# Two of seven inner tiles of the MLP by seven products ahead of the attention, and the output projection by seven products

## The chip, the cores and the metric

The kernel runs on one core of one Trainium2 chip. Its time is the device time of the core in microseconds (us); shorter is better. TensorE (PE) multiplies matrices into PSUM; VectorE (DVE), ScalarE (ACT) and GpSimd (POOL) work element by element; SyncE (SP) mostly issues DMAs, and so does ACT here for some stores. Each engine works through its own queue in order, and waits in it for what other engines or DMAs have to finish.

## The reference

One sequence of 2048 rows of width 1024, all in float32. The rows are normalized; attention with 32 heads of width 32 and an MLP with 3584 inner columns both start from the normalized rows, and the MLP's output gates the attention's.

```
xn = layernorm(x)
q, k, v = split(xn @ wqkv)                          # wqkv 1024 x 3072, 32 heads of 32
s = softmax(q k^T / sqrt(32)) v, heads joined, @ wo # wo 1024 x 1024
h = xn @ w1 + b1                                    # w1 1024 x 3584
g = silu((h * tanh(softplus(h))) @ w2)              # mish; w2 3584 x 1024
out = x + s * g
```

## The kernel before, in words

**Matmuls.** A float32 operand is split into a high part (a rounded copy, made by ACT, `copy`) and a low part (what is left, made by DVE or POOL, `low`). A product of two such operands is three matmuls: high by high, high by low, low by high (`THREE`). The unit of work is a matmul of 128 x 128 by 128 x 512 columns. The product of probabilities and v alone runs unsplit, four times slower for each pass, with four column groups at once.

**Stages.** (1) Rows are normalized and transposed, and v is made (`v_group`, L354); meanwhile POOL splits the first seven tiles of W1. (2) q and k (`product`, L798) are made by seven products in place of eight: the pair of a q and a k tile of 128 columns, times a pair of row chunks of 512, is taken as a 2 x 2 product of blocks in Winograd's form, with the inner dimension halved. Sums of weight blocks are made by POOL (`w_sum`, L554), split by ACT and DVE into pieces (`piece`), and sums of row blocks are prepared in stage 1. There are 16 jobs of seven products of twelve matmuls: eight column tiles for each of two pairs of row chunks. `q_load` brings a job's weights two jobs ahead; `SEQ` is the order of products; `out_` copies and splits a finished block and stores it to DRAM. After each product, `later.tick()` runs what was put off by some products. In the last five jobs the first head's scores (`s_mm`) run in between.

(3) The attention and the MLP run together, in an order that a planner works out on the host before the kernel is built (`Plan`). Five streams of PE work are given with a due time each (`key`): the scores s, by which a row's maximum is found (L920, DVE takes the maximum at L926); the transposed scores t (L1007), which ACT turns into exponentials p (L285); h (L1213), 24 matmuls for each of 28 inner tiles and 4 row chunks; y (L1303), the MLP's second product; and the output's first row chunk. The planner keeps a clock for every engine and takes on PE the operation that is ready and due first. Rings give the buffers: seven p tiles, one z, three `act`, five W2 halves (`w2`), two whole W1 tiles (`w1`). For each head, POOL adds up the p tiles into z (L1036), 15 additions; p times v runs on PE in three groups (`GROUPS`, L1054); then z's column sums (`zp`, L1080) and the division (`norm`), and the head's rows go to DRAM (`ot`, L1102). `mish` is five steps of ACT and seven of DVE for each h tile of 128 x 512, ending in a split `act`. W2 comes raw for the first row chunk, is split by ACT and POOL (L296) and stored for the other three; so are 21 tiles of W1. y is summed in `yacc` by DVE (L1325) and stored to `ys` at the end of each chunk (L1330).

(4) The output (L1402): 16 row tiles by two halves of columns, 24 matmuls each, 768 in all, followed by two DVE steps per block (L1495, L1496: times the gate, plus x). Its first eight blocks are the planner's fifth stream: their first half uses heads 0 to 15, stored long before, and their second half the rest. The gate is Silu of y, by ACT.

Of the kernel before, what the change touches and what calls it, by code (L numbers as in the profile page):

```python
# [18 lines left out]
P = 128  # L19
# [9 lines left out]
SLOW, UNTIL = 1.25, 700.0  # L29

W2_Q = 0
NS = H * NT
HK = KT // 2

# [6 lines left out]
PS, ACTS, W2S, Y0, Y1 = 7, 3, 5, 0.6, 0.17  # L41

AHEAD, BEHIND = 1.5, 1
# [4 lines left out]


# [3 lines left out]
LEAN = ("11875111088588544715468766661886741604280263056046486663654100588"  # L53
        "24308444562028442608686254255866647666488105044664767708017872000")
# [35 lines left out]
class Plan:  # L90
# [6 lines left out]
    SEM, SWITCH, LAND, RATE = 0.07, (0.25, 0.13), 2.0, 0.25e6  # L97
# [25 lines left out]
    def ready(self, op):  # L123
# [8 lines left out]
        for name in op.take:  # L132
            if not self.rings[name]:
                return None
            when = max(when, min(self.rings[name])[0] + self.SEM)
# [15 lines left out]
    def do(self, op, when):  # L151
# [8 lines left out]
        elif e == "SP":  # L160
            self.dma = max(self.dma, start) + op.bytes / self.RATE
            op.end = self.dma + self.LAND
        else:
            op.end = start + took
            took -= self.AHEAD[e]
# [65 lines left out]
def body(ctx: ExitStack, tc: tile.TileContext, x, wqkv, wo, w1, b1, w2, out):  # L231
# [17 lines left out]
    w1s = [dram.tile([P, 2, KT, P], F32R, name=f"w1s{i}") for i in range(FT)]  # L249
# [10 lines left out]
    nc.vector.memset(one, 1.0)  # L260
    zero = consts.tile([P, 1], F32, name="zero")
# [38 lines left out]
    def w1_tile(name):  # L300
        return w1p.tile([P, 2, KT, P], F32R, tag="w1", name=name, bufs=2)
# [132 lines left out]
    def split_w(w, raw, job=False):  # L434
        for half in range(2):
            r = slice(half * 4, half * 4 + 4)
            if job:
                nc.gpsimd.tensor_copy(w[:, 0, r], raw[:, r])
            else:
                copy(w[:, 0, r], raw[:, r])  # L440
            low(nc.gpsimd if job else nc.vector, w[:, 1, r], raw[:, r], w[:, 0, r])
# [4 lines left out]
    def w1_early():  # L446
# [3 lines left out]
        if f > 1:  # L450
            move(w1s[f - 2], early_w1.pop(f - 2)[1])
        if f < W1_V:
            raw = vp.tile([P, KT, P], F32, tag="x", name=f"w1e{f}", bufs=XB)
            nc.sync.dma_start(raw, w1[:, f * P:(f + 1) * P].rearrange("(k p) f -> p k f", p=P))
            early_w1[f] = [raw, None]
        if 0 < f <= W1_V:
            raw, _ = early_w1[f - 1]
            early_w1[f - 1][1] = w = w1_tile(f"w1p{f - 1}")
            split_w(w, raw, True)
# [75 lines left out]
    nc.sync.dma_start(bias1, b1.rearrange("(f p) -> p f", p=P))  # L535

    PAIRS = ((2, 3), (0, 1))
    A11, S2, A12, S3, S1, A22, S4 = range(7)
    NQ = 2 * KT
    raws, sums, pieces = {}, {}, {}  # L540

    def q_load(q, tiles, halves=range(2)):
        raws[q] = tiles
        for half in halves:
            col = half * D + q % KT * P
            nc.sync.dma_start(tiles[half], wqkv[:, col:col + P].rearrange("(k p) f -> p k f", p=P))
# [1014 lines left out]
```

## Time and profile before

| | before |
|---|---|
| median of 3 runs | 3362.83 us (3362.34 to 3363.39) |
| span of the profiled execution | 3358.0 us |
| PE busy | 3345.8 us |
| POOL busy | 2524.7 us |
| DVE busy | 2510.8 us |
| ACT busy | 2056.5 us |
| DMA, read and written in HBM | 352.55 and 144.97 MB |

The profiled execution's own time is known by its span, from the first to the last instruction; the runs' times are taken around the whole launch. In the profile, a group's row gives the line, the engine, the operation, the tile written and those read, how many there are, their busy time and the mean of one, and after the second bar the time in which the engine stood idle before them and what ended it. Matmuls overlap, so a mean of 391 ns says little; the step from one to the next says more. A row of the chain of work gives start, length and what ran. "DMA to landing" is from the issue to the data's arrival.

### The profile page before, as it was taken

What the parts mean: (1) busy time and instruction counts of PE and PEld (TensorE: products, weight loads), DVE (VectorE), ACT (ScalarE), POOL (GpSimd) and SP (SyncE); (2) the same over time, 40 slices, a digit from 0 to 9 for tenths busy, and PEclk for the clock granted to TensorE, in tenths of its full rate; (3) what the DMA queues carried; (4) which work ended last, traced back from release to release, by engine and by line L of the source; (5) the groups of instructions that cost most, each with busy time, mean ns of one, the idle gap of its engine ahead of it and who ended that gap; (6) DMA issues with size and microseconds to landing.
All of it is one profiled execution on the core that took longest, in us unless ns stands there. A gap on an engine that the chain in (4) does not pass through costs nothing.

```text
span 3358.0 us, 45795 instructions
## 1 busy us (share of the span) xinstructions
PE 3345.8 (100%) x16886; PEld 2458.4 (73%) x16886; DVE 2510.8 (75%) x3987; ACT 2056.5 (61%) x3313; POOL 2524.7 (75%) x750
## 2 busy tenths in 40 slices
PE   9999999999999999999999999999999999999999
PEld 7888887776777677776777677777677777767787
DVE  6665678877877778887888688888787888886542
ACT  5233436676766666666676666666667666667621
POOL 1323546999999887888888988888888898889800
PEclk9999999999999999999999999999999999999999
DMA  7865745454565643343335334333344433433482
GB/s 248 298 204 181 242 146 183 140 184 152 169 191 172 221 126 115 105 122 114 101 117 179 111 101 126 101 112 116 101 151 139 116 106 112 130 108 107 140 304 83
DMA packets 291460, 501.56 MB, mean 149 GB/s; under 512 B 88138, under 2 KB 151114, under 8 KB 269130
## 3 DMA queue, kind: packets, MB, share of 16 engines
q1 hardware_dynamic: 271524, 456.95, 43.8%
q10 hardware_dynamic: 19712, 41.69, 3.3%
q8 instruction: 133, 2.18, 0.3%
q14 instruction: 91, 0.75, 0.1%
HBM read 352.55 MB, written 144.97 MB: 148 GB/s over the span
## 4 chain that ended last, share of the span: by engine, by line
PE 96%; DMA 1%; DVE 1%; POOL 1%; issue 0%; ACT 0%; SPq 0%; ACTq 0%; POOLq 0%; DVEq 0%
PE y L1303 18%; PE h L1213 18%; PE t L1007 14%; PE s L920 13%; PE pv L1054 13%; PE op L1402 5%; PE v L354 5%; PE q_y L798 3%; PE q_z L798 2%; PE q_x L798 2%; PE zp L1080 1%; PE s L700 0%; POOL z L1036 0%; PE pt L423 0%; DMA w2r<-in_B_w_dram 0%
## 5 line engine op out<-in xcount | busy, mean ns | idle before, releaser
L1036 POOL TENSOR_TENSOR z<-z,p 128x2048 f32<-128x2048 f32 x448 | 2067.7, 4615 | 98.0 <-ACT p L285 72.9
L285 ACT ACTIVATE p<-t,zero 128x512 f32<-128x512 f32 x2048 | 1377.1, 690 | 560.1 <-PE t L1007 535.7
L926 DVE TENSOR_REDUCE mx<-s 128x1 f32<-128x512 f32 x1984 | 1322.3, 685 | 382.7 <-PE s L920 371.9
L1303 PE MATMUL y<-w,act 128*128 128x512 f32 x2688 | 920.3, 391 | 0.8 <-DVE yacc L1325 0.5
L1007 PE MATMUL t<-qstack,kstack 128*128 128x512 f32 x2048 | 799.1, 393 | 1.1 <-ACT p L285 0.7
L920 PE MATMUL s<-kstack,qstack 128*128 128x512 f32 x1984 | 772.6, 393 | 0.2 <-ACT p L285 0.2
L1213 PE MATMUL h<-xr,w 128*128 128x512 f32 x2016 | 697.7, 391 | 0.4 <-DMA xr<-xs 0.4
L1303 PEld LDWEIGHTS y<-w,act 128*128 128x128 f32 x2688 | 503.3, 188 | 114.3 <-issue 6.7
L1007 PEld LDWEIGHTS t<-qstack,kstack 128*128 128x128 f32 x2048 | 383.8, 188 | 114.8 <-issue 18.0
L1054 PE MATMUL pv<-p,v 128*32 128x512 f32 x4096 | 459.3, 594 | 0.0
L920 PEld LDWEIGHTS s<-kstack,qstack 128*128 128x128 f32 x1984 | 369.6, 188 | 118.5 <-issue 32.1
L1213 PEld LDWEIGHTS h<-xr,w 128*128 128x128 f32 x2016 | 378.3, 188 | 81.2 <-issue 3.4
L1325 DVE TENSOR_TENSOR yacc<-yacc,y 128x512 f32<-128x512 f32 x416 | 282.7, 680 | 82.6 <-PE y L1303 81.5
L1054 PEld LDWEIGHTS pv<-p,v 128*32 128x32 f32 x4096 | 123.3, 110 | 282.7 <-issue 281.1
L1036 POOL TENSOR_TENSOR z<-p,p 128x2048 f32<-128x2048 f32 x32 | 148.1, 4628 | 185.2 <-PE zp L1080 146.6
L1213 PE MATMUL h<-xc,w 128*128 128x512 f32 x672 | 231.3, 391 | 1.3 <-DMA w<-w1s 1.0
L354 PE MATMUL v<-vw,xc 128*128 128x512 f32 x768 | 179.7, 392 | 1.2 <-ACT xc L288 0.7
L354 PEld LDWEIGHTS v<-vw,xc 128*128 128x128 f32 x768 | 142.7, 188 | 32.0 <-ACT xc L288 1.4
L1213 PEld LDWEIGHTS h<-xc,w 128*128 128x128 f32 x672 | 125.9, 188 | 30.5 <-issue 2.5
L288 ACT ACTIVATE act<-h 128x512 fp32r<-128x512 f32 x112 | 66.6, 595 | 88.2 <-DVE h L1262 87.0
L798 PE MATMUL q_y<-xc,wq 128*128 128x512 f32 x480 | 115.3, 389 | 0.0
L798 PEld LDWEIGHTS q_y<-xc,wq 128*128 128x128 f32 x480 | 90.0, 188 | 18.8
(149 smaller groups left out, 2947.4 us busy)
## 6 DMA issues: line engine op xcount, KB each, us to landing
w<-w1s SPq DMA_DIRECT2D x91, 1024.0 KB, 5.4
w<-w2s SPq DMA_DIRECT2D x168, 512.0 KB, 4.0
w2s<-w SPq DMA_DIRECT2D x56, 512.0 KB, 4.0
qstack<-qs SPq DMA_DIRECT2D x96, 256.0 KB, 6.3
kstack<-ks SPq DMA_DIRECT2D x96, 256.0 KB, 5.8
w1s<-w SPq DMA_DIRECT2D x21, 1024.0 KB, 5.8
qs<-qst ACTq DMA_DIRECT2D x32, 512.0 KB, 4.1
ks<-qst ACTq DMA_DIRECT2D x32, 512.0 KB, 3.7
```

Of the source, the lines that this page charges most:

```text
L285: nc.scalar.activation(out_, in_, fn, bias=zero if bias is None else bias, scale=scale)
L354: nc.tensor.matmul(ps, xc[t // 4][k // HK][:, a, k % HK, (t % 4) * P:(t % 4 + 1) * P], vw[i, k // 2][:, b, k % 2], start=n == 0, stop=n == ...
L798: nc.tensor.matmul(ps, w[:, a, k], xx[:, b, k], start=m == 0 and i in (0, 1, 4), stop=m == 3 * HK - 1, skip_group_check=i not in (0, 1, 4))
L920: nc.tensor.matmul(sp_, qst[h % 3][:, qt * P:(qt + 1) * P], kst[h % 3][:, kc * 512:(kc + 1) * 512], start=True, stop=True)
L926: nc.vector.reduce_max(tiles["mx"][:, qt, kc:kc + 1], tiles[qt, kc], axis=AX.X)
L1007: nc.tensor.matmul(tp, kst[h % 3][:, kt * P:(kt + 1) * P], qst[h % 3][:, c * 512:(c + 1) * 512], start=True, stop=True)
L1036: nc.gpsimd.tensor_tensor(zs[h], pts[T - 1] if kt == 1 else zs[h], pts[T], ALU.add)
L1054: nc.tensor.matmul(pv[h][c * DH:(c + 1) * DH, :], vt[h][:, k, :], pts[T - kt + k][:, c * 512:(c + 1) * 512], start=k == 0, stop=k == NT - 1)
L1213: nc.tensor.matmul(t["h"], w1t[n][:, a, k], xts_[c][k // HK][:, b, k % HK], start=i == 0, stop=i == 3 * KT - 1)
L1303: nc.tensor.matmul(t["y"], acts[n][:, p, s * P:(s + 1) * P], w2t[m_][:, q], start=j == 0 and i == 0, stop=j == YB - 1 and i == 2)
L1325: nc.vector.tensor_tensor(ya, ya, t["y"], ALU.add)
L1402: nc.tensor.matmul(ps[t, dh], ohl[t // 4, k][:, a, s * P:(s + 1) * P], wt[k][:, b, r], start=k == 0 and i == 0, stop=k == KT - 1 and i == 2)
```

## The change

Three things, and what they carry along.

**Seven products for part of h.** Of 28 inner tiles, those with number 2 or 5 modulo 7 (`MADE`, eight) leave the attention. They are made in stage 2: two such tiles are the two column blocks of a job, in the place that a q and a k tile have, and eight jobs (four pairs by two pairs of chunks) stand between the two halves of the q/k jobs. Of each block, `out_` stores to DRAM (`hs`) the two things that mish needs, e = exp(min(h, 12)), as exp(12 - relu(12 - h)), and (e + 2) e h. In the attention such a tile is loaded (`h_load`, ring `hb`) and its mish starts from there, with four steps of ACT and four of DVE. The other tiles' mish takes the minimum on ACT (`a0`) in place of DVE (`d1`).

**W2 and the W1 buffers.** 38 of the 56 half-tiles of W2 are split in stage 2 (`ahead`, one each three or four products: load, copy by ACT, low by POOL, store). In the attention, the lows of the remaining W2 halves and W1 tiles move from POOL to DVE. The room of two whole W1 tiles becomes four quarters: in the attention two of them hold W1 in halves (`HALVES`), one holds `e`, one the loaded h. The ring of v shrinks from two to one, that of `act` grows to four.

**The output by seven products.** Eight jobs of 256 rows by 1024 columns, seven products of twelve matmuls each, after the attention. wo's block sums are made by POOL and split as the planner's fifth stream; the rows' sums by DVE and POOL. The planner's due times leave `END` = 30 us between the end of t and the end of all, `SLOW` is 1.0 in place of 1.25, and the string `LEAN`, which shifts the planner's choices in each 21 us, is another.

```diff
-SLOW, UNTIL = 1.25, 700.0
-W2_Q = 0
+SLOW, UNTIL = 1.0, 700.0
+NP = NT // 2
+MADE = [f for f in range(FT) if f % 7 in (2, 5)]
+KEPT = [f for f in range(FT) if f not in MADE]
-PS, ACTS, W2S, Y0, Y1 = 7, 3, 5, 0.6, 0.17
-AHEAD, BEHIND = 1.5, 1
+PS, ACTS, W2S, Y0, Y1 = 7, 4, 5, 0.6, 0.17
+AHEAD, BEHIND, END, H0 = 1.5, 1, 30.0, 1.0
+LOWS, W2_Q = "DVE", 38
...
-    def w1_tile(name):
-        return w1p.tile([P, 2, KT, P], F32R, tag="w1", name=name, bufs=2)
+    def quarter(i, name, shape=(P, 2, HK, P), dtype=F32R):
+        return w1p.tile(list(shape), dtype, tag=f"quarter{i}", name=name)
...
-    NQ = 2 * KT
+    NM = len(MADE) // 2
+    JOBS = [("q", t) for t in range(KT)] + [("h", g) for g in range(NM)] * 2 + [("q", t) for t in range(KT)]
+    NQ = len(JOBS)
+    TURN_Q, OFF = NQ // 2, NM
...
     def out_(q, half, chunk_, src):
+        kind, t = JOBS[q]
         st = sp.tile([P, 2, 512], F32R, tag="qst", name=f"qst{q}_{half}_{chunk_}", bufs=4)
+        if kind == "h":
+            f = MADE[2 * t + half]
+            dst = hs[f].rearrange("h p n -> p h n")[:, :, chunk_ * 512:(chunk_ + 1) * 512]
+            e, num = st[:, 0].bitcast(F32), st[:, 1].bitcast(F32)
+            def first():
+                act(num, src, AF.Relu, bias=rest1[:, f:f + 1], scale=-1.0)
+                act(e, num, AF.Exp, bias=twelve, scale=-1.0)
+            def second():
+                nc.vector.scalar_tensor_tensor(src, src, bias1[:, f:f + 1], e, op0=ALU.add, op1=ALU.mult)
+                nc.vector.scalar_tensor_tensor(num, e, 2.0, src, op0=ALU.add, op1=ALU.mult)
+            later.at(1, first)
+            later.at(2, second)
+            later.at(4, lambda: nc.scalar.dma_start(dst, st.bitcast(F32)))
+            return
...
+    def ahead(n):
+        f, d = divmod(n, 2)
+        raw = prep[0].tile([P, 512], F32, tag="wraw", name=f"wraw{n}")
+        nc.sync.dma_start(raw, w2[f * P:(f + 1) * P, d * 512:d * 512 + 512])
+        def high():
+            splits[n] = prep[0].tile([P, 2, 512], F32R, tag=f"wsp{n % TWO[0]}", name=f"wsp{n}")
+            copy(splits[n][:, 0], raw)
+        def rest():
+            low(nc.gpsimd, splits[n][:, 1], raw, splits[n][:, 0])
+        later.at(2, high)
+        later.at(3, rest)
+        later.at(4, lambda: move(w2s[f][:, :, d * 512:d * 512 + 512], splits[n]))
...
-        return UNTIL * SLOW + (t - UNTIL) * (total - UNTIL * SLOW) / (total - UNTIL)
+        return UNTIL * SLOW + (t - UNTIL) * (total - END - UNTIL * SLOW) / (total - UNTIL)
...
+    def h_load(n, need):
+        c, f = divmod(n, FT)
+        t = {}
+        def emit(at):
+            t["in"] = quarter(1, f"h{n}", (P, 2, 512), F32)
+            nc.sync.dma_start(t["in"], hs[f].rearrange("h p n -> p h n")[:, :, c * 512:(c + 1) * 512])
+        t["own"] = op("SP", 0.1, need=need, emit=emit, take=["hb"], bytes_=P * 1024 * 4)
+        return t
...
+        while "h" not in final:
+            yield None
+        u0 = split(0, [b11, final["h"]], ["xc0"])
+        t2 = sum_("T2", [u0, t3])
+        u1 = split(1, [t2, final["h"]], ["xc1"])
+        u2 = split(2, [b21, final["h"]], ["w1", "w1", "hb", "e", "e"])
+        t4 = sum_("T4", [u2, t2])
...
+        a0 = op("SP", 0.1, need=[final[H - 1], stored[H - 1]], bytes_=P * S * 4,
+                emit=lambda at: a_load(0, home("q", i0, "araw0")))
...
     ph = ExitStack()
-    op_ = pool(ph, "op", 8)
...
+    tl = pool(ph, "tl", 1)
...
+    def raw_tile(j):
+        return tl.tile([P, S], F32, tag="araw", name=f"araw{j}", bufs=2)
+    WIDE = [("k", i0), ("q", i0), ("q", i2), ("k", i2), ("q", i1), ("k", i1)]
...
+    def out_load(j):
+        set_, p = jobs[j]
+        outs[j, "g"] = wide(f"g{j}", 2 * p, WIDE)
+        nc.sync.dma_start(outs[j, "g"], ys[p // 2][:, p % 2 * 2:p % 2 * 2 + 2])
+        outs[j, "x"] = wide(f"x{j}", 2 * p + 1, WIDE)
+        nc.sync.dma_start(outs[j, "x"], x[p * 256:p * 256 + 256, :].rearrange("(t p) d -> p t d", p=P))
...
+        if i == 4:
+            tt(G, g, e, g, ALU.mult)
+            tt(G, xx, xx, g, ALU.add)
+        elif i == 2:
+            tt(V, g, ps, g, ALU.mult)
+            tt(V, xx, xx, g, ALU.add)
         else:
+            tt(G, e, e, g, ALU.mult)
+            tt(G, xx, xx, e, ALU.add)
+            tt(V, g, ps, g, ALU.mult)
+            tt(V, xx, xx, g, ALU.add)
...
+    a_load(1, raw_tile(1))
+    for which, eng in (("S1", nc.vector), ("S2", nc.vector), ("S3", nc.gpsimd)):
+        a_sum(0, which, eng, small(f"0{which}", which))
+    b_sum("o", "T1", nc.gpsimd)
+    b_high("o", 3)
...
+    for j in range(last + 1):
+        for i in range(7):
+            mm7(j, i)
+            nxt = j + 1
+            if j == 0:
+                if i < 6:
+                    a_unit(0, i + 1)
+                if i == 0:
+                    b_low("o", 3, nc.vector)
+                if 0 < i < 4:
+                    b_unit("o", i + 3)
+            after(j, i)
             later.tick()
+            if nxt <= last:
+                if i == 1:
+                    for which in ("S1", "S2", "S3"):
+                        a_sum(nxt, which, nc.gpsimd, small(f"{nxt}{which}", which))
+                later.at(LAG, lambda nxt=nxt, i=i: a_unit(nxt, i))
+            if i == LAG and j + 2 <= last:
+                a_load(j + 2, raw_tile(j + 2))
+            if i == 1 and j == 0:
+                out_load(j)
+            if i == 3 and nxt <= last:
+                out_load(nxt)
+            if i in (2, 3):
+                t = i - 2
+                act(outs[j, "g"][:, t], outs[j, "g"][:, t], AF.Silu)
+            if i >= 4:
+                for n in {4: (4,), 5: (2, 5), 6: (6,)}[i]:
+                    done(j, n)
```

In the last part, `mm7` issues a product's twelve matmuls, `a_unit` splits a block of rows or of their sums (copy by ACT, low by DVE), `b_unit` one of wo's (on four times the width), `a_load` brings a job's rows of all heads from `ot` (eight DMAs, one for each inner tile), and `done` finishes an output block. A product takes what `a_unit` and `b_unit` made for it.

More of the change, by code (lines that the diff above doesn't have):

```diff
@@ L990, in p_done @@
         if len(uses[T]) == 2:
-            plan.give("p", max(o.end for o in uses[T]))
+            plan.give("p", max(o.end for o in uses[T]), by=exps[T][0])
     def t_stream():
@@ L1142, in rest, with high @@
[L1142 to L1148 removed]
+            def high(at, half=half):
+                copy(w1t[n, half][:, 0], w1r[n, half])
```

546 lines of the change are left out of this document (303 added, 243 removed).

## The prediction

> **What bounds the kernel now.** I read the page's busy times and its chain first, then the waits of TensorE, then the busy times by stage, the groups of instructions, and last the order of time around the end of the attention. Shares of the span first, with a stage of the attention below them (length, then busy time of PE, PEld, DVE, ACT, POOL, the granted clock, the DMA share, GB/s):
>
> ```profile
> span 3358.0 us, 45795 instructions
> PE 3345.8 (100%) x16886; PEld 2458.4 (73%) x16886; DVE 2510.8 (75%) x3987; ACT 2056.5 (61%) x3313; POOL 2524.7 (75%) x750
> ```
> ```profile
> 720.00:1100.00 380.00, 378.44 (x1926) 273.36 (x1925) 299.18 (x476) 266.01 (x436) 362.83 (x135) 1.00 0.56 176
> ```
>
> TensorE never rests, and POOL is second: 75% of the span, 95% of this stage. A busy PE is pipelined, so what says it is at its pace is the chain, where twelve matmuls of 512 columns follow each other in 2.72 us, 0.2267 each:
>
> ```profile
> 200.19 2.72 PE q_x L798 x12
> ...
> 3158.50 13.64 PE y L1303 x60
> ...
> 3179.26 174.11 PE op L1402 x768
> ```
>
> 60 y in 13.64 and 768 op in 174.11 give the same 0.227. So time is the number of matmuls, unless PE begins to wait. The stages: q/k from 200.2, attention from 521.1 (next row), output from 3179.3.
>
> ```profile
> 521.09 0.62 PE L920 MATMUL s<-kstack,qstack 128*128 128x512 f32 x2
> ```
>
> **What goes.** The change touches two groups:
>
> ```profile
> L1213 PE MATMUL h<-xr,w 128*128 128x512 f32 x2016 | 697.7, 391 | 0.4 <-DMA xr<-xs 0.4
> L1213 PE MATMUL h<-xc,w 128*128 128x512 f32 x672 | 231.3, 391 | 1.3 <-DMA w<-w1s 1.0 <-ACT p L285 0.3
> L1402 PE MATMUL op<-wo,xo 128*128 128x512 f32 x384 | 87.4, 389 | 0.0
> L1402 PE MATMUL op<-wo,ohl 128*128 128x512 f32 x384 | 87.4, 389 | 0.0
> ```
>
> h has 2688 matmuls: 28 tiles x 4 chunks x 24. Eight of 28 leave the attention: 768 fewer, 174.1 us. They come back in the q/k stage as 8 jobs x 7 products x 12 = 672, 152.3 us. The output has 768; 8 jobs x 7 x 12 = 672 replace them. Both together: 192 matmuls, **-43.5 us**. The attention, 3179.3 - 521.1 = 2658.2 us, should shrink to 2484, the q/k stage grow by 152, the output take 152.3 instead of 174.1. Everything else in the sum is a wait that PE doesn't have now.
>
> **The q/k stage: +1.5.** An h job has q's loads, sums and splits, and in place of each of four copies and lows two activations on ACT and two three-operand steps on DVE, nearest in price:
>
> ```profile
> L285 ACT ACTIVATE e<-e,zero 128x512 f32<-128x512 f32 x112 | 80.5, 719 | 34.2 <-DVE e L1233 33.8
> L1243 DVE SCALAR_TENSOR_TENSOR h<-h,bias,e 128x512 f32<-128x512 f32 x112 | 84.3, 752 | 12.2 <-ACT e L285 11.5
> L296 POOL TENSOR_TENSOR w<-w2r,w 128x512 fp32r<-128x512 f32 x56 | 72.5, 1295 | 32.6 <-ACT w L288 32.6
> L296 POOL TENSOR_TENSOR w<-w1r,w 128x512 fp32r<-128x512 f32 x42 | 54.5, 1297 | 4.6 <-ACT w L288 4.1 <-DMA w2r<-in_B_w_dram 0.5
> 200.00:312.00 112.00, 112.00 (x495) 92.44 (x494) 60.39 (x90) 39.05 (x69) 33.01 (x24) 1.00 0.60 192
> ```
>
> Per job of 19.0 us that adds at most 4 x 0.75 = 3.0 us of DVE to 10.3 (60.39 of 112), and 4 x 0.72 to ACT's 6.6. One W2 half-tile in three products (8.2 us) adds 1.3 us to POOL, which is busy 33 of 112. SP gets two more issues there, ahead of the q loads. All stay below 75%, so PE hides it. No job of this kind is in the trace: nothing at least (PE doesn't wait in that row), 8 at most if each h job waits 1 us. I take 1.5, nearer to the row.
>
> **The attention's own waits: +5.** PE's waits there now are few; the largest, and two kinds of load (KB each, us to landing):
>
> ```profile
> PE h L1213 <- DMA w<-w1s: 1.0, 1, 1.0
> ```
> ```profile
> w<-w1s SPq DMA_DIRECT2D x91, 1024.0 KB, 5.4
> w<-w2s SPq DMA_DIRECT2D x168, 512.0 KB, 4.0
> ```
>
> W1 is held in two half tiles instead of two whole ones. A half of 512 KB lands in about 4.0 us, like w2s; it is needed after the other half's twelve matmuls, which in the even order span 15 us (2484 us / 160 halves) but in a burst 2.72. So a burst can expose 4.0 - 2.7 = 1.3 us. I take four such, 5 us; ends 0 and 13 (ten). DVE loses more than it gets: 32 x 3 mish steps of 0.75 (72 us), against the lows of 13 W1 tiles and 18 W2 halves, 44 of 0.69 (its row stands below; 30 us).
>
> **The output's start: +18.3, and the end: +2.4.** Now the first output products use heads stored long before, and cover the last head. After the change the first product needs a sum over all heads' rows. Last head's path now:
>
> ```profile
> 3105.10 66.82 POOL L1036 TENSOR_TENSOR z<-z,p 128x2048 f32<-128x2048 f32 x14
> 3181.31 0.33 SPq L1330 DMA_DIRECT2D ys<-yacc  x1
> ...
> 3191.97 0.34 SPq L1350 DMA_DIRECT2D or<-ot  x1
> 3192.42 3.70 SPq L1478 DMA_DIRECT2D oraw<-ot  x8
> 3195.50 0.63 ACT L288 ACTIVATE xo<-or 128x512 fp32r<-128x512 f32 x1 [3.00 <-DMA or<-ot]
> 3196.17 0.69 DVE L296 TENSOR_TENSOR xo<-or,xo 128x512 fp32r<-128x512 f32 x1 [2.25 <-ACT xo L288]
> 3206.04 1.28 ACT L285 ACT_TABLE_LOAD   x1 [9.91 <-DMA y<-ys]
> 3207.34 1.15 ACT L285 ACTIVATE y<-y,zero 128x1024 f32<-128x1024 f32 x1
> ```
>
> From the last addition's end, 3171.9, to split data, 3196.9, pass 25 us. END leaves t 30 us earlier, so that y covers most of it; I charge nothing for this path, and up to 10 in the range.
>
> What PE meets next is the gate's load. The new pool opens where the pool with yacc stood; yacc is the first tile there (16 KB a partition), and the two raw tiles of the output (2 x 8 KB) are the first in the new one. So the load of job 1's raw tile, next on SP, waits until yacc is stored, and behind it on SP stands the gate's load, for which job 0's Silu waits on ACT, and behind Silu the split for product 4. From the last y, E (first the landing in the view of the tile yacc, then two kinds of transfer):
>
> ```profile
> DMA to landing us min/median/max: 7.4/7.4/7.4
> ```
> ```profile
> y<-ys SPq DMA_DIRECT2D x16, 512.0 KB, 8.3
> ys<-yacc SPq DMA_DIRECT2D x4, 2048.0 KB, 10.4
> ```
>
> addition 0.7 + issue 0.3 + the last store's landing 7.4 + 8 issues 3.7 + landing 8.3 (y, half as large) + table load 1.3 + Silu 1.15 + split 0.6 + 0.7 = E + 24.2. Undisturbed, product 4 starts at E + 4 x 2.72 = 10.9: **+13.3**. With 3.5 (the or load) as its landing it is 8.5; with 10.4 for both landings 18.4. Product 5's split then stands on ACT behind a split of wo (four times 0.63), one of job 1 and the second Silu: 2.5 + 0.63 + 1.15 + 0.63 = 4.9 against a product's 2.72, **+2.2**. After such a pause PE starts slowly, as it did at the very start:
>
> ```profile
> 1.82 7.14 PE L473 MATMUL idle<-xc 128*128 128x512 f32 x19 [1.82 <-POOL xc L470]
> ```
> ```profile
> 3.50:7.00 3.50, 3.50 (x9) 2.72 (x9) 2.25 (x7) 1.14 (x3) 0.00 (x0) 1.00 0.96 325
> ```
>
> 19 x 0.2267 is 4.3, so 2.8 is lost, although the granted clock says 1.00; I take **+2.8** (0 if the clock row is right). The Trainium skill (TensorE: Matmul & The Clock Gate, Part 1: The HAM clock gate) says that about 3.4 us without work puts the array back to half clock; the first matmuls' spacing agrees, the clock column doesn't, and by that rule the charge recurs with each long pause.
>
> The end: product 4, 5 and 6 leave POOL six two-input steps of 1.3, done 0.7 + 7.8 = 8.5 us after product 4, when PE is through at 5.4; then one DVE step. Now two DVE steps follow PE: 9.2 against 6.8, **+2.4**. The ends are 0 and 4.
>
> **Sum.** 3358.0 - 43.5 + 1.5 + 5 + 13.3 + 2.2 + 2.8 + 2.4 = 3341.7. The three runs' median lies 4.8 over the profiled span, so **3346.5 us**.
>
> **Rivals.** *The output starts unhindered* (y's last blocks end early, or the gate lands in time): without 13.3 + 2.2 + 2.8 it is 3328, with no waits in the attention 3323. For it: POOL's last additions, not y, may end last. Against: the store of yacc waits for the last y in any order.
>
> *POOL sets the pace* (slower). Its additions:
>
> ```profile
> L1036 POOL TENSOR_TENSOR z<-z,p 128x2048 f32<-128x2048 f32 x448 | 2067.7, 4615 | 98.0 <-ACT p L285 72.9
> L1036 POOL TENSOR_TENSOR z<-p,p 128x2048 f32<-128x2048 f32 x32 | 148.1, 4628 | 185.2 <-PE zp L1080 146.6 <-ACT p L285 38.6
> ```
> ```profile
> 534.72 3.98 POOL z L1036
> ```
>
> Busy 2215.8, waits for zp 146.6 (one z buffer), small gaps 25.1: 2387.5 that can't shrink. With 13.6 of start and 25 of the last head's path it is 2426 of 2484. Its waits for exponentials, 111.5 now, may reach 58 unseen; if all stay, data comes 53 late. Then y ends early and the gate's wait is covered: 3358 - 43.5 + 1.5 + 5 + 53 + 2.8 + 2.4 + 4.8 = 3384. It turns into a loss from about 90 of the 111.5. For it: POOL has 58 us of room instead of 232. Against: 98 lows (127 us) leave POOL, and t is due earlier. The Trainium skill (GPSIMD Engine Reference, Specifications) says that DVE steps with two SBUF inputs contend with POOL, and 44 lows become such; by it the floor would rise by up to 44 x 0.69 = 30. No row of the attention isolates that.
>
> *Half tiles of W1 are late* as a rule: 1.3 us in 12 halves more than counted is 16, or 3362, no change.
>
> **How the numbers follow.** Forecast 0.52, unhindered output 0.25, late W1 0.10, POOL 0.13. About 0.2% (6.7 us) is what a measurement can tell. Faster: the first two and a third of the W1 case, 0.80; the rest of that case and a little of POOL's is no change, 0.08; slower 0.12. The range goes from 3323 (unhindered) to 3368 (the forecast with the upper ends of the q/k stage, 6.5, of the attention, 8, and of the landing, 5.1; the W1 case lies within) and leaves out POOL's case.
>
> **What would show it.** Right: h with 1920 matmuls in the attention and 672 in L798's line, 672 op; an attention of about 2490 us; in the output one PE wait of 8 to 18 us before product 4 of job 0, its chain yacc, ys, SP, y, Silu. Wrong: POOL's z waiting less than 60 us while PE waits for stored heads; PE waits in h for w1s above 15 us; or PE gaps in the q/k stage above 8.

## The result: slower by 3.5%, and the profile after

The changed kernel takes 3479.82 us (median of four runs, 3478.49 to 3482.66) beside 3363.11 before: a ratio of 1.035, 95% interval [1.033, 1.036]. The forecast was 3346.5, with a range that ended at 3368. The profiled execution took 3480.56, its span is 3478.8. First the page after: the span, and busy time of each engine.

```profile
span 3478.8 us, 46380 instructions
PE 3364.8 (97%) x16694; PEld 2436.7 (70%) x16694; DVE 2669.0 (77%) x4051; ACT 2163.3 (62%) x3505; POOL 2646.0 (76%) x804
...
PE 79%; DVE 7%; DMA 4%; issue 4%; POOL 3%; ACT 1%; SPq 0%; POOLq 0%; ACTq 0%; DVEq 0%
```

PE runs 16694 matmuls where it ran 16886: the 192 are gone, as counted. But PE is no longer busy all the time; it idles 114 us of the span (before: 12), and in the chain that ended last (third row) DVE now holds 7%.

Where the time went is read stage by stage: from the first start of each stage's products, with the forecast's own terms put to the same stages (us).

| stretch | before | forecast | after | after less forecast |
|---|---|---|---|---|
| up to the first q product | 200.0 | 200.0 | 201.1 | 1.1 |
| q/k stage | 321.1 | 474.9 | 493.6 | 18.7 |
| attention | 2658.0 | 2488.9 | 2592.2 | **103.3** |
| output and end | 178.9 | 177.8 | 191.9 | 14.1 |
| span | 3358.0 | 3341.7 | 3478.8 | 137.1 |

The attention by row chunks: in the view of windows, its first chunk (694.7 to 1371), and the other three. Columns: length, busy time of PE, PEld, DVE, ACT, POOL, the granted clock, the DMA share, GB/s.

```profile
694.70:1371.00 676.30, 629.10 (x3132) 428.84 (x3131) 573.18 (x823) 451.89 (x730) 543.48 (x123) 0.97 0.42 123
1371.00:3286.90 1915.90, 1896.99 (x9894) 1325.24 (x9894) 1495.31 (x2363) 1352.28 (x2168) 1710.49 (x395) 1.00 0.43 125
```

PE idles 47 us in the first chunk and 19 in the rest, and only the first shows a lower granted clock. The view of waits says what PE waited for in the attention:

```profile
PE s L988 <- DVE mx L994: 24.5, 14, 3.8
PE h L1319 <- DMA w<-w1s: 15.0, 9, 3.9
PE t L1073 <- DVE mx L994: 8.9, 4, 3.6
PE y L1433 <- DVE yacc L1455: 4.5, 3, 2.6
PE t L1073 <- DVE act L1386: 4.2, 3, 3.2
```

Apart from W1's loads these five are all DVE. DVE is busy 573 of 676 us there, which leaves it 15%; but two groups of its steps are long. From the groups by line, with the mean in ns as the last number ahead of the second bar:

```profile
L306 DVE TENSOR_TENSOR w<-w1r,w 128x512 fp32r<-128x512 f32 x26 | 51.4, 1977 | 14.6 <-ACT w L298 14.6
L306 DVE TENSOR_TENSOR w<-w2r,w 128x512 fp32r<-128x512 f32 x18 | 45.3, 2516 | 1.3 <-ACT w L298 1.1
L306 DVE TENSOR_TENSOR vw<-vraw,vw 128x512 fp32r<-128x512 f32 x16 | 10.3, 688 | 7.4 <-ACT vw L298 7.3
```

All three are the same step on the same shape. The last, ahead of the attention, takes 0.688 us; the moved lows take 1.98 and 2.52, together 66 us more than 44 x 0.69. One of them in the view of order of time (start, length), DVE first, then POOL, then PE:

```profile
1087.08 3.50 DVE L306 TENSOR_TENSOR w<-w1r,w 128x512 fp32r<-128x512 f32 x1
1090.50 0.69 DVE L1368 SCALAR_TENSOR_TENSOR q<-q,r 128x512 f32<-128x512 f32 x1
1091.10 0.68 DVE L994 TENSOR_REDUCE mx<-s 128x1 f32<-128x512 f32 x1
```
```profile
1085.43 9.55 POOL L1104 TENSOR_TENSOR z<-z,p 128x2048 f32<-128x2048 f32 x2
```
```profile
1091.83 0.67 PE L988 MATMUL s<-kstack,qstack 128*128 128x512 f32 x1 [2.85 <-DVE mx L994]
...
1094.00 1.05 PE L1433 MATMUL y<-w,act 128*128 128x512 f32 x2
1094.85 0.63 PE L1073 MATMUL t<-qstack,kstack 128*128 128x512 f32 x1
```

The first of POOL's two additions takes 4.60 and ends at 1090.03. The low comes while it runs and ends at 1090.58, 0.55 after it. The other lows behave alike: of the 44, 13 begin while POOL does nothing and take 0.68 or 0.69; 30 begin within a POOL addition and end 0.55 to 0.65 after that addition, wherever in it they began. The one left begins together with an addition, and there it is the addition that is long (DVE, then POOL):

```profile
1253.78 0.68 DVE L306 TENSOR_TENSOR w<-w1r,w 128x512 fp32r<-128x512 f32 x1
```
```profile
1253.77 5.17 POOL L1104 TENSOR_TENSOR z<-z,p 128x2048 f32<-128x2048 f32 x1
```

Behind the low of 1087.08, in DVE's queue, stands a maximum that PE's score bank needs, and PE stands still for 2.85. Then its matmuls follow each other in 0.43 (two y and a t in 1.28) where 0.227 is its pace, for about 3.5 us; the granted clock from 1091 to 1099 is 0.79. The Trainium skill (TensorE: Matmul & The Clock Gate, Part 1: The HAM clock gate) lets the array fall to half clock after a window of about 3.4 us without work; here 2.85 was enough to see it. So a late low costs PE its wait and can cost a slow stretch besides: in the attention PE's idle time grew by 62 us over before, and its busy time is 46 more than before's less the 768 matmuls that left.

### The profile page after: what moved, and what is told of

It reads as the page before. It is cut to its first block, busy times and chain, and to the rows that moved or that the text cites. A ratio compares the mean times of both kernels' runs of the same rounds, so it can differ in the third digit from the quotient of the medians.

```text
span 3478.8 us, 46380 instructions
## 1 busy us (share of the span) xinstructions
PE 3364.8 (97%) x16694; PEld 2436.7 (70%) x16694; DVE 2669.0 (77%) x4051; ACT 2163.3 (62%) x3505; POOL 2646.0 (76%) x804
## 4 chain that ended last, share of the span: by engine, by line
PE 79%; DVE 7%; DMA 4%; issue 4%; POOL 3%; ACT 1%; SPq 0%; POOLq 0%; ACTq 0%; DVEq 0%
PE y L1433 17%; PE pv L1122 12%; PE t L1073 12%; PE s L988 12%; PE h L1319 11%; PE v L364 5%; PE q_y L857 3%; PE q_x L857 2%; PE q_z L857 2%; DVE w L306 2%; DMA w<-w1s 2%; DVE mx L994 2%; POOL ws L571 1%; PE zp L1148 1%; DMA wraw<-in_B_w_dram 1%
## 5 line engine op out<-in xcount | busy, mean ns | idle before, releaser
L1073 PE MATMUL t<-qstack,kstack 128*128 128x512 f32 x2048 | 804.2, 397 | 17.4 <-DVE mx L994 8.9
L988 PE MATMUL s<-kstack,qstack 128*128 128x512 f32 x1984 | 781.2, 398 | 25.5 <-DVE mx L994 24.5
L1319 PE MATMUL h<-xr,w 128*128 128x512 f32 x1440 | 501.6, 394 | 12.1 <-DMA w<-w1s 12.1
L1319 PEld LDWEIGHTS h<-xr,w 128*128 128x128 f32 x1440 | 271.4, 189 | 74.8 <-DMA w<-w1s 15.3
L857 PE MATMUL q_y<-xc,wq 128*128 128x512 f32 x720 | 173.8, 390 | 2.7 <-ACT wq L298 1.4
L1319 PE MATMUL h<-xc,w 128*128 128x512 f32 x480 | 168.2, 397 | 5.1 <-DMA w<-w1s 3.0
L857 PEld LDWEIGHTS q_y<-xc,wq 128*128 128x128 f32 x720 | 134.6, 188 | 33.2 <-issue 2.6
L857 PE MATMUL q_z<-xc,wq 128*128 128x512 f32 x576 | 140.4, 393 | 6.8 <-DVE e L842 6.8
L857 PE MATMUL q_x<-xc,wq 128*128 128x512 f32 x576 | 139.1, 390 | 4.6 <-ACT wq L298 2.6
```

The source lines that it names most:

```text
L857: nc.tensor.matmul(ps, w[:, a, k], xx[:, b, k], start=m == 0 and i in (0, 1, 4), stop=m == 3 * HK - 1, skip_group_check=i not in (0, 1, 4))
L988: nc.tensor.matmul(sp_, qst[h % 3][:, qt * P:(qt + 1) * P], kst[h % 3][:, kc * 512:(kc + 1) * 512], start=True, stop=True)
L1073: nc.tensor.matmul(tp, kst[h % 3][:, kt * P:(kt + 1) * P], qst[h % 3][:, c * 512:(c + 1) * 512], start=True, stop=True)
L1319: nc.tensor.matmul(t["h"], w1t[n, k // HK][:, a, k % HK], xts_[c][k // HK][:, b, k % HK], start=i == 0, stop=i == 3 * KT - 1)
```

## The experiments

Theory P: a DVE step that reads two operands in SBUF stands until the step that POOL is in has ended. Its rivals: the late W1 halves, PE's gate alone, or DVE simply having too much to do. Each run stands beside runs of the kernel before on the same chip (medians 3360.8 to 3362.8). The stages are of the profiled execution; "first" and "rest" are the attention's first row chunk and the other three, parted at the first h of the second chunk.

| run | time (median) | q/k | first | rest | output |
|---|---|---|---|---|---|
| before | 3363.11 | 321.1 | 593.0 | 2065.0 | 178.9 |
| changed | 3479.82 | 493.6 | 678.8 | 1913.4 | 191.9 |
| e1 memset for the lows | 3406.41 | 494.3 | 609.5 | 1912.5 | 194.0 |
| e2 before, lows on DVE | 3494.32 | 321.0 | 718.7 | 2072.4 | 178.8 |
| e3 lows read PSUM | 3455.71 | 494.5 | 624.9 | 1945.6 | 187.4 |
| e4 no work on W2 ahead | 3464.94 | 481.2 | 675.6 | 1909.6 | 193.5 |
| e5 lows on POOL again | 3478.95 | 494.2 | 641.5 | 1953.7 | 189.7 |
| e6 sixth operand first | 3480.42 | 494.1 | 686.0 | 1907.5 | 191.0 |
| e7 DVE's last steps put off | 3468.03 | 494.2 | 676.6 | 1916.4 | 180.9 |
| e8 e1, W1 not loaded again | 3397.11 | 493.6 | 609.3 | 1897.9 | 194.0 |
| e9 W2 ahead by POOL | 3472.36 | 484.0 | 685.9 | 1913.4 | 194.6 |
| e10 all five out | 3367.98 | 481.2 | 609.9 | 1897.6 | 179.4 |
| e11 repaired | 3437.42 | 482.4 | 622.7 | 1948.8 | 177.3 |
| e12 small low first | 3482.24 | 495.4 | 677.9 | 1912.3 | 194.6 |
| e13 e12, Silu later | 3483.05 | 494.2 | 679.9 | 1915.9 | 191.0 |

(Before, a "first" chunk holds 672 h matmuls, after 480.) Kernels with the same attention (changed, e4, e6, e7, e9, e12, e13) differ in it by up to 14 us, 2585 to 2599, so a stage's own length tells more than the total where a term is small.

**e1: the lows without their operands.**

```diff
-low(nc.vector if LOWS == "DVE" else nc.gpsimd, w1t[n, half][:, 1], w1r[n, half], w1t[n, half][:, 0])
+nc.vector.memset(w1t[n, half][:, 1].bitcast(F32), 0.0)
...
-low(nc.vector if LOWS == "DVE" else nc.gpsimd, w2t[m][:, 1], w2r[m], w2t[m][:, 0])
+nc.vector.memset(w2t[m][:, 1].bitcast(F32), 0.0)
```

> The changed kernel, with the 26 W1 and 18 W2 lows of the attention's first row chunk (DVE, two SBUF operands) replaced by a DVE memset of the same tile at the same place in the same order; the low parts of those tiles are left zero, which leaves that part of the products out. All loads, buffers, POOL work and PE work stay. Theory P (a DVE step that reads two SBUF operands waits for the step that POOL is in, and PE waits behind DVE's queue): the attention falls from 2592 us to 2500-2530, nearly all of it before 1371 us, PE's waits for mx and act fall by over half, time 3390-3420. Rival W1 (the smaller raw buffers of W1 and their loads set the pace) and rival C (PE is only slower because of the gate, whatever DVE does): the attention stays at 2580-2595, time 3465-3485.

The attention took 2522.0, 70 less, and the first chunk alone 69 less. (The profile is of the slower of e1's two executions, 3412.34 and 3400.47.) In the windows of e1:

```profile
694.60:1303.00 608.40, 603.40 (x3135) 419.66 (x3134) 509.79 (x825) 451.05 (x731) 532.00 (x123) 1.00 0.46 138
```

The same work (3135 matmul records for 3132, 123 steps of POOL), PE idle for 5 us instead of 47, and the clock at 1.00: the gate was a consequence. PE's waits for mx are 0.8. What is left of PE's waits is W1's loads:

```profile
PE h L1319 <- DMA w<-w1s: 15.4, 8, 4.0
PE t L1073 <- ACT p L295: 1.6, 4, 0.5
PE s L988 <- DVE mx L994: 0.8, 2, 0.6
```

A memset reads nothing and is 0.2 us shorter than a quiet low (0.485), which gives 44 x 0.2 = 9 us of DVE at most. It also doesn't wait for ACT's copy, for which DVE stood 15.7 us ahead of the lows in the changed kernel. The rest needs another cause, and the next two runs show which.

**e2: that one step put into the kernel before.**

```diff
-low(nc.gpsimd, w1t[n][:, 1, r], w1r[n, half], w1t[n][:, 0, r])
+low(nc.vector, w1t[n][:, 1, r], w1r[n, half], w1t[n][:, 0, r])
...
-low(nc.gpsimd, w2t[m][:, 1], w2r[m], w2t[m][:, 0])
+low(nc.vector, w2t[m][:, 1], w2r[m], w2t[m][:, 0])
```

The planner is told of the move too (0.72 us on DVE for 1.3 on POOL), so its order is made anew.

> The kernel before, with only the lows of the weights W1 and W2 in the attention (98 of them) moved from POOL to DVE, nothing else of the change. Theory P: DVE's lows take 1.5 us and more instead of 0.7 wherever POOL runs beside them, the first row chunk grows, and the time is 3420-3520. Rival (the lows cost their 0.7 us on DVE, and POOL is relieved): 3340-3385.

3494.32, 1.040 times before [1.037, 1.043], worse than the whole change. The attention grew by 133 us, 126 of them in the first chunk, and no W1 half tile, no h by seven products and no new output is in this kernel. Its groups:

```profile
L296 DVE TENSOR_TENSOR w<-w2r,w 128x512 fp32r<-128x512 f32 x56 | 130.0, 2321 | 3.7 <-ACT w L288 3.5
L296 DVE TENSOR_TENSOR w<-w1r,w 128x512 fp32r<-128x512 f32 x42 | 73.9, 1759 | 1.0 <-ACT w L288 1.0
```

98 lows take 203.9 us and not 68: 136 too many, and the attention is 133 longer. The loss is about as large as the lows' extra length, as in the changed kernel (66 and 70). Again 34 lows begin while POOL does nothing and take 0.67 to 0.69, and the other 64 end 0.54 to 0.66 after the POOL step that they began in.

**e3: the same step with one operand in PSUM.**

```diff
 copy(w1t[n, half][:, 0], w1r[n, half])
+ps_[0] = bank(at, f"w1q_{n}_{half}").rearrange("p (k f) -> p k f", f=P)
+copy(ps_[0], w1r[n, half])
...
-low(nc.vector if LOWS == "DVE" else nc.gpsimd, w1t[n, half][:, 1], w1r[n, half], w1t[n, half][:, 0])
+low(nc.vector, w1t[n, half][:, 1], ps_[0], w1t[n, half][:, 0])
...
```

The same is done for W2.

> The changed kernel, all of the result computed, with the 44 lows kept on DVE but reading the raw piece from a PSUM bank that ACT writes (44 more ACT copies and bank uses), so that no low reads two SBUF operands. The planner's order moves with it and is by its own clock 42 us longer (2556 for the attention instead of 2514). Theory P: the lows take 0.65-0.8 us each and hardly ever wait for POOL, the attention takes 2550-2580 and the time is 3435-3465, less than the changed kernel in spite of the longer plan. Rival (DVE's queue is late for its load, not for the port): lows of the same length or a longer attention than 2592, time 3480-3530.

All of the result is computed, and 24 us of the loss are gone. The lows of e3 by their tile (minimum, median and maximum in ns) beside those of the changed kernel:

```profile
L306 DVE TENSOR_TENSOR w<-w1q,w x26: 678/680/692, 882.8 to 1302.5; 128x512 fp32r<-128x512 f32 x26
L306 DVE TENSOR_TENSOR w<-w2q,w x18: 679/682/693, 1138.3 to 1407.8; 128x512 fp32r<-128x512 f32 x18
```
```profile
L306 DVE TENSOR_TENSOR w<-w1r,w x26: 681/882/4884, 882.1 to 1338.2; 128x512 fp32r<-128x512 f32 x26
L306 DVE TENSOR_TENSOR w<-w2r,w x18: 676/2834/5008, 1157.7 to 1424.8; 128x512 fp32r<-128x512 f32 x18
```

Same engine, output and size, but never above 0.693 us where it was up to 5.0, although 37 of the 44 begin within a POOL step; and these lows still wait for a copy by ACT (4.9 us). That settles P against "DVE has too much to do". The first chunk is 54 shorter, the rest 32 longer; the planner had given this order 42 us more by its own clock, since it counts ACT's second copy and the banks. The Trainium skill says this outright (SBUF — State Buffer, SBUF: two separate sides): DVE and GpSimd share one pair of ports as an exclusive lock; a GpSimd step or a DVE step with two SBUF inputs, whichever starts first, has it for its whole instruction, and the other blocks. The traces agree, with up to 5.0 us for one step. "The lock" below is this wait of one engine for the other's step.

**e4 and e9: the q/k stage.** Its PE waits are small in number, and ACT's queue shows why they are there. From the waits of ACT in that stage of the changed kernel, and of PE:

```profile
ACT wsp L298 <- DMA wraw<-in_B_w_dram: 92.6, 30, 10.1
```
```profile
PE q_z L857 <- DVE e L842: 6.8, 5, 4.3
PE q_x L857 <- ACT wq L298: 2.6, 1, 2.6
PE q_y L857 <- DVE e L842: 2.4, 3, 1.2
```

ACT stands 92.6 us at the head of its queue for W2's raw pieces, with the copy of a product's first sum (e) and of weights (wq) behind it. e4 leaves that work out (two plain copies in DRAM stand in for it), e9 gives ACT's part to POOL:

```diff
-raw = prep[0].tile([P, 512], F32, tag="wraw", name=f"wraw{n}")
-nc.sync.dma_start(raw, w2[f * P:(f + 1) * P, d * 512:d * 512 + 512])
+for a in range(2):
+    nc.sync.dma_start(w2s[f][:, a, d * 512:d * 512 + 512].bitcast(F32), w2[f * P:(f + 1) * P, d * 512:d * 512 + 512])
+return
```

> The changed kernel, where the q/k stage's work for W2 is only two copies of the raw piece from DRAM to DRAM (no ACT copy, no POOL low, no wait of either; the split of those W2 pieces is left out). Theory Q (ACT stands at the head of its queue waiting for the raw piece of W2, 92.6 us in 30 waits, and the evacuations behind it come late to PE): the q/k stage falls from 493.6 to 474-482 us, time 3462-3472. Rival (the stage is longer because of the seven products' own evacuations): the stage stays at 490-495, time 3476-3484.

```diff
-copy(splits[n][:, 0], raw)
+nc.gpsimd.tensor_copy(splits[n][:, 0], raw)
```

> The changed kernel, all of the result computed, with the high part of W2's ahead-of-time pieces copied by POOL instead of ACT, so that it is POOL that stands waiting for the raw piece. Theory Q (only ACT's standing still matters, not the work): the q/k stage falls from 493.6 to 479-485 us, time 3465-3474. Rival (W2's pieces cost the stage by their bytes or by POOL's work beside DVE): 488 or more.

The stage falls from 493.6 to 481.2 and to 484.0, and PE's q_z wait for e from 6.8 to 1.8 and 1.5: theory Q holds, it was ACT's standing still and not the work. e9's total is unsteady (3465.57 and 3479.14); in the profiled one the later stages gave the gain back, for which no cause was looked for. About 6 us over the forecast's stage remain in e4. They are not explained.

**e5: the lows on POOL again.**

```diff
-LOWS, W2_Q = "DVE", 38
+LOWS, W2_Q = "POOL", 38
```

> The changed kernel with the 44 lows of the attention on POOL again, as before the change, all else kept; the planner makes its order anew (its own clock gives the attention 2584 us instead of 2514, because it counts 1.3 us on a POOL that is 82-85% busy there). Theory P with the planner's clock: no low waits, but POOL is full in the first row chunk; the attention takes 2585-2625 us, PE waits for POOL's z and not for mx, time 3470-3510, so going back on this part alone regains nothing. Rival (the rest of the change left POOL room enough): attention 2500-2540, time 3390-3430.

No gain: 3478.95. The lows take 1.29 us each on POOL and the first chunk is 37 us shorter, but the other three are 40 longer, in an order that the planner made anew. In those three PE idles 39 us and not 19, and is busy 20 longer for the same work. In the attention PE's longest waits are 12.1 for W1's loads and 8.9 for mx, not for POOL's z as expected. So the lows had a reason to leave POOL in this kernel, by the planner's clock; what makes the 40 us was not followed.

**e8: W1 not loaded again.** Added to e1:

```diff
+        if n >= FT:
+            w1t[n, half] = w1was[at]
+            return
```

> The kernel of the first experiment (memset for the 44 lows), and besides the W1 halves of the row chunks 1 to 3 are not loaded again: their products read whatever half tile lies in the buffer, so the h products of those chunks are left wrong in value and the same in number, order and length. It prices the change's third part, W1 in two half buffers. If the 12 us of PE's waits for these loads, and the slower clock that follows a wait, are what is left over 2484-2489 us: the attention falls from 2522 to 2490-2505 us. Rival (the load hides another wait that comes next, for act or p): it stays above 2512.

The attention falls by 14.8 to 2507.2, all in the three later chunks (1912.5 to 1897.9), a little less than expected; the medians differ by 9.3, with e1's two times 12 apart. The other kernels of this order have 1907.5 to 1916.4 in those chunks, so the fall there is more than their spread. PE's waits for these loads fall from 15.4 to 2.9, the new longest is 4.0 for act: some of the wait was covering another.

**e7: the output's steady state.** A job takes 20.38 us and not 19.04. From the groups of the output stage of the changed kernel, DVE's column of waits:

```profile
L1646 DVE TENSOR_TENSOR g<-op_y,g 128x512 f32<-128x512 f32 x8 | 5.5, 692 | 20.6 <-POOL e L1646 20.6
```
```profile
PE op_y L1641 <- DVE e L1646: 11.7, 8, 3.7
```

DVE waits 2.6 us in each job for POOL's sum, and behind that step stands the sum that frees PE's bank.

```diff
-tt(V, g, ps, g, ALU.mult)
-tt(V, xx, xx, g, ALU.add)
+def rest():
+    tt(V, g, ps, g, ALU.mult)
+    tt(V, xx, xx, g, ALU.add)
+if j == len(jobs) - 1:
+    rest()
+else:
+    later.at(2, rest)
...
-later.at(2, lambda: nc.sync.dma_start(out[r:r + P, :], outs[j, "x"][:, t]))
+later.at(4, lambda: nc.sync.dma_start(out[r:r + P, :], outs[j, "x"][:, t]))
```

> The changed kernel with DVE's last two steps of products 5 and 6 of each output job put off by two products, so that they do not hold up the evacuations that PE needs while they wait for POOL's sum. If DVE's queue standing behind POOL is what makes a job take 20.38 us instead of 19.04, jobs fall to 19.0-19.4 us, the output stage from 191.9 to 182-185, time 3470-3476. Rival (each output step is itself late, by POOL beside DVE or by ACT): jobs stay above 20 us, stage 189-193.

The stage is 180.9, 11 less and a little under what was expected, and a job takes 19.04; in e7 PE's wait for that sum is 2.7 us in the whole stage:

```profile
PE op_y L1641 <- DVE e L1646: 2.7, 2, 1.7
```

**e6, e12, e13: the output's start.** Product 4 of the first job (the fifth, as they count from 0) starts 20.4 us after the first in the changed kernel; without waits it would be 10.9. Three runs took suspects away, and none shortened the stage by more than 1 us.

```diff
-        t = tl.tile([P, 2, HK, 512], F32R, tag=f"u{i}", name=f"{set_}u{i}")
+        t = u6_ if i == 6 else tl.tile([P, 2, HK, 512], F32R, tag=f"u{i}", name=f"{set_}u{i}")
...
+    u6_ = tl.tile([P, 2, HK, 512], F32R, tag="u6", name="ou6")
```

> The changed kernel with the sixth output operand given its memory first, so that the second gate load no longer stands behind the store of the y sums. If the chain that was read from the trace holds, product 4 of the output starts 12 to 15 us after the output's first product (20.4 in the changed kernel) and the output stage falls from 191.9 to 183-187 us, time 3471-3476. Rival (it is the split of that operand, or PE's slow clock at the start, whatever the load): 18 us or more, output stage 189-193.

Missed: 19.2 us. SP's wait for the store falls from 5.9 to 1.1 us, but the eight raw loads now take 7.4 to issue and not 3.6 (up to 1.3 for one of them, 0.4 in the changed kernel), and the gate's load leaves SP 10.6 us after the first product (11.0 in the changed kernel). And another wait hid this one all along. In e6, the third product's operand and the step ahead of it, POOL's sum, and PE:

```profile
3292.73 6.65 DVE L306 TENSOR_TENSOR ou<-ob,ou 128x2048 fp32r<-128x2048 f32 x1
3299.31 0.68 DVE L306 TENSOR_TENSOR a<-araw,a 128x512 fp32r<-128x512 f32 x1
```
```profile
3292.22 5.01 POOL L1485 TENSOR_TENSOR ob<-ob,ob 128x2048 f32<-128x2048 f32 x1
```
```profile
3300.04 3.88 PE L1642 MATMUL op_x<-ou,a 128*128 128x512 f32 x10 [4.12 <-DVE a L306]
```

Again the lock: POOL's sum ends at 3297.23, the low needs 2.28 elsewhere and ends at 3299.38. e12 lets the small low go first, e13 also moves Silu behind the splits:

```diff
                     a_unit(0, i + 1)
-                if i == 0:
+                if i == 1:
                     b_low("o", 3, nc.vector)
```

> The changed kernel with one line of the output stage put one product later: the low of output operand 3 (DVE, two SBUF operands, 128x2048) is issued behind the low that product 3 of the first job (third in order) waits for, not ahead of it. If DVE standing till POOL's sum ends (6.66 us for that low, 2.28 elsewhere) is what holds the third product: it starts 5.5 to 7.5 us after the first and not 10.5. If the gate's load stands behind that (ACT waits for it up to 17.2 us after the first product, and the split that product 5 in order needs stands behind it): that product still starts at 18 to 21 us, and the output stage stays at 188-192 us. If the lock alone is the delay: it starts at 13 to 15 us, stage 184-187.

```diff
-            if i in (2, 3):
-                t = i - 2
+            for t in ((0, 1) if i == 4 else ()) if j == 0 else ((i - 2,) if i in (2, 3) else ()):
                 act(outs[j, "g"][:, t], outs[j, "g"][:, t], AF.Silu)
```

> As the experiment before it, and the first job's two Silu steps are issued one and two products later on ACT, behind the splits of products 5 and 6 in order, so that ACT no longer stands waiting for the gate ahead of them. If the two chains (the lock and the gate) each cover for the other: product 5 starts 12 to 15 us after the first, output stage 182-187 us, time 3470-3476. If a third thing holds it: 18 us or more.

Product 4 starts 23.2 (e12) and 18.1 us (e13) after the first, the times are 3482.24 and 3483.05: e12 is later than either case expected, and e13's 18.1 is what had been put down to a third thing. In e12 the small low took the lock's wait in place of the large one:

```profile
3291.49 4.78 DVE L306 TENSOR_TENSOR a<-araw,a 128x512 fp32r<-128x512 f32 x1 [0.20 <-ACT a L298]
3296.20 5.57 DVE L306 TENSOR_TENSOR ou<-ob,ou 128x2048 fp32r<-128x2048 f32 x2
```

Whichever low comes during POOL's 5 us sum stands till it ends. Behind these rows stands, in DVE's queue, the sum that frees PE's bank, and PE waits 3.6 for it in e12. In e13 the gate is out of the way. PE's rows of e13, from the third product on:

```profile
3299.99 3.84 PE L1641 MATMUL op_x<-ou,a 128*128 128x512 f32 x10 [1.96 <-DVE a L306]
3306.18 3.08 PE L1641 MATMUL op_y<-ou,a 128*128 128x512 f32 x12 [2.35 <-DVE e L1646]
3309.10 2.96 PE L1641 MATMUL op_z<-ou,a 128*128 128x512 f32 x12
```

Product 4 (op_z) starts without a wait of its own, and the waits for DVE ahead of it (0.3, 2.0 and 2.4) with the slower matmuls behind them still give 18 us. The gate alone was not run; in the changed kernel its load lets ACT go on 17.4 us after the first product, so by the trace it would hold product 4 to about 20 us without any lock. That each chain hides the other is shown for the first and argued for the second. A kernel without that POOL sum was not tried.

**e10 and e11: all of it together.** e10 is e8, e4, e6 and e7 at once; e11 computes the whole result, with e3, e9, e6 and e7.

> All five suspects out of the changed kernel at once: memset for the 44 lows, W1 not loaded again in chunks 1 to 3, W2's pieces moved without ACT and POOL, the sixth operand's memory first, DVE's last steps put off. Values are left wrong in the parts that the single experiments name. If the five are separate and are the whole story, the time is the changed kernel's 3480 less about 70, 20, 12, 7 and 9, that is 3355-3370; the forecast's own sum was 3342-3347. If one hides another, or something is left unnamed, it is above 3375.

> The changed kernel, all of the result computed, with the lows read from PSUM (third experiment), W2's high parts copied by POOL, the sixth operand's memory first and DVE's last steps put off. By the single effects 3456 less about 10, 7 and 9: 3425-3435, still slower than before, since the order is the planner's for other costs (42 us by its own clock) and W1's half tiles stay.

```profile
682.00:3189.40 2507.40, 2494.35 (x13025) 1742.73 (x13024) 1996.34 (x3185) 1801.16 (x2897) 2244.85 (x518) 1.00 0.36 104
```

e10 takes 3367.98 (eight runs), its stages are those of the single runs to within 2 us: the effects add up. Of 137 us over the forecast its span of 3368.9 leaves 27, of which 18.6 lie in the attention (PE idles 13 of the 2507.4, before 4) and 6 in the q/k stage. Even so, and with parts of the work left out, it stands at 1.002 of before [1.001, 1.003]. e11 is 3437.42, 1.023 [1.020, 1.026]: just over the 3425 to 3435 expected, and no gain over before. No version here beats the kernel before.

## Why the prediction was wrong

**What held.** The matmuls: 1920 h and 672 op as counted, 672 more in L857, 192 fewer in all. No row speaks against the 43.5 us they are worth. W1's half tiles are late as the term and its rival told, only the size was off: taken at 5, up to 13, and 16 more in the rival; 15.0 us of waits in the trace, 14.8 by e8's profile. POOL did not set the pace: in the first chunk it is busy 80%, less than the 95% before. The gate's chain in the output (yacc, store, loads, gate, Silu, split) is there in the order told. (The upper end of the range, 3368, is 2 more than its own terms give: 3346.5 + 6.5 + 8 + 5.1 = 3366.1.)

**The step that failed** is in the attention's own waits: "DVE loses more than it gets: 32 x 3 mish steps of 0.75 (72 us), against the lows of 13 W1 tiles and 18 W2 halves, 44 of 0.69". It priced a step that moves to another engine by a row of that engine in which the other one stood still. The row taken, a split of xo at 3196.17, begins 24 us after POOL's last addition. Its own group in the trace of before, by tile, and one of its members with POOL's additions beside it, would have said it:

```profile
L296 DVE TENSOR_TENSOR xo<-or,xo x8: 679/760/2865, 3164.8 to 3196.2; 128x512 fp32r<-128x512 f32 x8
```
```profile
3164.83 2.62 DVE L296 TENSOR_TENSOR xo<-or,xo 128x512 fp32r<-128x512 f32 x1
```
```profile
3156.68 15.25 POOL L1036 TENSOR_TENSOR z<-z,p 128x2048 f32<-128x2048 f32 x3
```

The three additions end at 3161.3, 3166.9 and 3171.9; the low of 2.62 ends at 3167.45, 0.55 after the second. DVE's other steps in the attention of before give no hint, since mish keeps h and q in PSUM banks, yacc's second operand is in PSUM and a maximum has one operand. An estimate from rows: POOL adds for 4.63 us and is busy 80% of the chunk, so a low that comes at any time waits 0.8 x 4.63 / 2 = 1.85 on average; measured were 96.7 / 44 - 0.69 = 1.51. 44 x 1.85 = 81 us, beside the 70 of e1.

**The contention was seen, and only half of it priced.** The rival with POOL named the Trainium skill's rule that such steps contend (GPSIMD Engine Reference, Specifications), and charged POOL with it: "by it the floor would rise by up to 44 x 0.69 = 30". DVE's wait, the larger part, since POOL's step is seven times as long, got no price, and "No row of the attention isolates that" should have widened the range instead of closing the matter.

**The q/k stage, +1.5:** 18.7 over it. The sum looked at how busy each engine is ("All stay below 75%, so PE hides it"), not at what a queue waits for. ACT's new copy waits for a DMA, in order, and evacuations stand behind it: 12.4 by e4. The bound given, 8, was passed too: PE idles 15.3 us there.

**The output, 14.1 over it:** the steady state was missed. The forecast took two DVE steps to follow PE at the end alone and saw no wait for POOL's sum in each of the other jobs: 11 us by e7. The start was told in part: product 4 is 9.5 late and not 13.3, but not by the one wait of 8 to 18 us ahead of it that the forecast named. PE waits 4.2 there for a low that the lock holds, which no term had, and 1.2 for the split behind the gate. That the size came near is luck.

**Open:** 27 us of e10 over the forecast. PE idles 6.3 us more than before in the q/k stage and 9.3 in the attention, where the forecast had 1.5 and 5: that is 9 of the 27. Another 14 is PE's busy time in the attention, 2494.4 against 2480.2 (before's less 768 x 0.2267); e10's mean granted clock is 0.996 where before has 1.000, which over its span would be about 13 us, an estimate. What causes either was not traced.

## What to carry to other kernels

Before a step is moved to another engine, look where its operands lie and what runs beside it there: two operands in SBUF on DVE, while POOL works through long steps, cost a third of a POOL step on average here (1.51 of 4.63 us), and an engine's in-order queue hands that on to whoever waits behind. Take a price from the group's minimum, median and maximum, not from one quiet instance, and read a busy share as a bound on work, never on waits: a step that waits for a DMA at the head of a queue can cost more than the step. And when a forecast knows of a contention that no row isolates, it belongs into the range with a price on both parties.

## What the runs showed of the hardware that was not expected

- The lock holds for an instruction at a time: the same DVE step takes 0.68 to 0.69 us with one operand in PSUM and up to 5.0 with both in SBUF beside POOL's 4.6 us additions. POOL is held as well: at the output's start of the changed kernel a step of it, where one of the same shape takes 1.30 (last row), comes just behind a DVE low and ends 1.1 us after that low, 3.26 after its own start (DVE first, then POOL).

```profile
3297.93 2.28 DVE L306 TENSOR_TENSOR ou<-ob,ou 128x2048 fp32r<-128x2048 f32 x1
```
```profile
3298.09 3.26 POOL L1529 TENSOR_TENSOR araw<-araw,0S 128x512 f32<-128x512 f32 x1 [2.83 <-DVE a L306]
...
3308.09 1.30 POOL L1529 TENSOR_TENSOR 1S<-araw 128x512 f32<-128x512 f32 x1 [6.74 <-DVE a L306]
```

- After a pause of 2.85 us PE's matmuls run for about 3.5 us at 0.43 instead of 0.227 each; the granted clock shows 0.79 from 1091 to 1099, and 0.97 over that chunk. The length of the pause alone does not decide it: after one of 2.13 us (at 1286.0) they are 0.43 apart for about 3 us, after one of 3.22 (at 1185.6) they are 0.23 apart at once.
